# Four attention layers on one core: layer-norm statistics behind each tile's addition, normalising inside the transposing piece, and a shorter Newton step

## The chip, the core and the metric

The kernel runs on one core of one Trainium2 chip. The core has a matrix engine (TensorE, "PE" in the profile), a vector engine (VectorE, "DVE"), an activation engine (ScalarE, "ACT"), a general engine (GpSimd, "POOL") and a sync engine (SyncE, "SP") that issues nearly all DMAs of this kernel. Every engine works through its own list of instructions in order and waits at semaphores for the others. The metric is the time of the whole launch on the device, in microseconds (us); lower is better.

## The reference

The input is x, 2048 tokens of 512 numbers. Four layers follow each other; layers 0 and 2 use the weights A and a sliding window, layers 1 and 3 use the weights B and full attention. Each layer is

```
n   = (x - mean) / sqrt(var + 1e-5)          # layer norm over the 512 numbers of a token
q, k, v = split(n @ wqkv)                    # 32 heads of 16
s   = q @ k^T * 0.25                         # layers 0, 2: token i sees tokens i-255 .. i only
x   = x + softmax(s) @ v @ wo
```

and the result is x after the fourth layer. The attention itself is most of the work: 32 heads times 2048 x 2048 scores in the full layers, an eighth of that or less in the window layers.

## The kernel before

**Tiling.** Tokens are cut into four chunks of 512 (`c` = 0 to 3), each of four tiles of 128 (`i` = 0 to 3). Heads are taken in eight groups of four (`qd`) and in four groups of eight (`t` or `ht`). Operands of the projections are split in two float16 parts (high and low), so that a 512-wide product takes 12 matmuls (4 slices of the inner dimension, 3 terms). The scores are computed transposed on PE (L649), ACT takes the exponential (L653), in the window layers POOL masks the two edges (L715, L718), and PE multiplies with the values (L693 in full layers, L725 in window layers).

**The works beside the attention.** What prepares the next layer is written as works, each cut into pieces by `yield`:

- OO(l, c), `wo` (L557 to L572): loads the four x tiles of the chunk (`load_x`), then for each tile 12 matmuls (po), the scaling by gcol (dx, L567), the addition (L568) and the store to `xd` (L569); after the last tile it calls `norm`.
- `norm` (L393 to L411): for each tile bn_stats (L398) and bn_aggr (L399), then the reciprocal root of the four variances by `rsqrt` (L41 to L52: three starting operations and three Newton steps of four operations, all on 128x4), then for each tile xn (L405, float32), xh (L405, float16) and the low part (L408).
- T(l, c), `transpose` (L422 to L436): for each tile 8 PE transposes into one PSUM bank (pt, L429), a copy of the high half by ACT or DVE (L432, L434) and of the low half by DVE (L435).
- K, Q, VV: projections of the transposed chunk `xc` to keys, queries and values (48 matmuls each, pq and pv). For layer 3 they are cut into quarters, K3 and Q3 (12 matmuls).
- NN(c) (L934): the same for layer 0, whose x comes from the input. PR: preparation of a weight matrix (DVE and POOL, much of it during layer 0).

**What sets the order.** PE's order is written out when the kernel is built: the code runs under `tc.manual_schedule` for PE alone, and a planner keeps an estimated time `clock[0]`. It emits one attention step (scores, and the product of an earlier step with the values), and after a step takes pieces of the current works list until their planned share is spent. A piece may say `yield "wait", t`: then its work isn't taken again before `clock[0]` has reached t. These planned waits are not waits of the chip; they only decide where a piece stands in PE's list. On the chip PE stops where the data of the next instruction isn't there. T's first tile waits for `XNR` = the planner's time at the end of `norm` plus 10, and each further tile for 2.3 more. Behind the last chunk of a window layer come the `tails` (layer 0: OO(0,3), VV(1,2), Q(1,1), T(1,3), K(1,3); layer 2: OO(2,3), VV(3,1), VV(3,2), Q3(0,0), T(3,3), K3(3,0)), which have no attention steps between them: there the planner takes the first work of the list that is ready, and if none is, the one that is ready first, and sets its clock to that time. A projection waits 8 after its weights' load was issued (`yield wait(8)`).

The orders of DVE, ACT, POOL and SP come from a scheduler that places each instruction by its own cost estimates and the order in which the code emitted them, with `high_priority` for the copy that frees an attention bank (L599). So a change in the emission order can move instructions against each other on DVE and SP too.

**Buffers.** There are 4 x tiles (`XB`), 3 pairs of high and low parts (`XNB`), one xn, three score banks (tag "s") which the works share for their own products, and in full layers a second accumulator. A new norm may only begin when the T of the chunk before it is done.

Of the kernel before, what the change touches and what calls it, by code (L numbers as in the profile page):

```python
# [9 lines left out]
F32 = mybir.dt.float32  # L10
BF16 = mybir.dt.bfloat16
F16 = mybir.dt.float16
# [3 lines left out]
ALU = mybir.AluOpType  # L16
AX = mybir.AxisListType

S, D, H, DH, WIN = 2048, 512, 32, 16, 256
P = 128  # L20
# [13 lines left out]
EB, XB, XNB, WB, VB, OB = 6, 4, 3, 2, 3, 5  # L34
# [4 lines left out]
def rsqrt(nc, vp, tag, var):  # L39

    v = vp.tile([P, 4], F32, name=f"v{tag}", tag="lnv")  # L41
    y = vp.tile([P, 4], F32, name=f"y{tag}", tag="lny")
    z = vp.tile([P, 4], F32, name=f"z{tag}", tag="lnz")
    nc.vector.tensor_scalar_add(v, var, EPS)
    nc.vector.tensor_scalar(y.bitcast(I32), v.bitcast(I32), 1, None, op0=ALU.logical_shift_right)
    nc.vector.tensor_scalar(y.bitcast(I32), y.bitcast(I32), -1, 0x5F3759DF, op0=ALU.mult, op1=ALU.add)
    for _ in range(3):
        nc.vector.tensor_mul(z, y, y)
        nc.vector.tensor_mul(z, z, v)
        nc.vector.tensor_scalar(z, z, -0.5, 1.5, op0=ALU.mult, op1=ALU.add)  # L50
        nc.vector.tensor_mul(y, y, z)
    return y  # L52


# [135 lines left out]
def fast_path(ctx, tc, flag, a_x, a_wqkv, a_wo, b_wqkv, b_wo, out):  # L190
# [3 lines left out]
    nc = tc.nc  # L194
# [3 lines left out]
    vp = pool("work", 2)  # L198
# [7 lines left out]
            for ty in range(2) for s in range(4)}  # L206

    XC, XN, V, O, KM, EP, PH = {}, {}, {}, {}, {}, {}, {"full": False}
    CM, DN, WT, pend = {}, {}, {}, []

    clock, DONE, XNR, ONR = [0.0], {}, {}, {}

    def spent(us):
        clock[0] += us
        return us

    def wait(us):

        return "wait", clock[0] + us
# [19 lines left out]
    xd = dp.tile([NT, P, D], F32, name="xd")  # L239
# [125 lines left out]
    def weights(ty, s, n, t=None):  # L365

        w = wp.tile([P, NC, 2, D], F16, name=f"w{n}", tag="w", bufs=WB)
        if t is None:
            nc.sync.dma_start(w, wd[ty, s])
            return w  # L370
        nc.sync.dma_start(w[:, :, :, :P], wd[ty, s][:, :, :, t * P:(t + 1) * P])
        return w

    def bank(name):

        if PH["full"]:
            return acc[1]
        return ps_s.tile([P, 2, QC], F32, name=name, tag="s")[:, 0, :]
# [11 lines left out]

    def norm(l, c, xs):  # L393

        st = vp.tile([P, 4, 6], F32, name=f"st{l}_{c}", tag="st")
        mv = vp.tile([P, 4, 2], F32, name=f"mv{l}_{c}", tag="mv")
        for i in range(4):
            nc.vector.bn_stats(st[:, i, :], xs[i])  # L398
            nc.vector.bn_aggr(mv[:, i, :], st[:, i, :])  # L399
        y = rsqrt(nc, vp, f"{l}_{c}", mv[:, :, 1])  # L400
        out = []
        for i in range(4):
            xn = vp.tile([P, D], F32, name=f"xn{l}_{c}_{i}", tag="xn", bufs=1)
            xh = vp.tile([P, 2, D], F16, name=f"xh{l}_{c}_{i}", tag="xh", bufs=XNB)
            norm1 = lambda o: nc.vector.tensor_scalar(o, xs[i], mv[:, i, 0:1], y[:, i:i + 1], op0=ALU.subtract, op1=ALU.mult)  # L405
            norm1(xn)
            norm1(xh[:, 0])
            nc.vector.tensor_tensor(xh[:, 1], xn, xh[:, 0], ALU.subtract)  # L408
            out.append(xh)
        XNR[l, c] = clock[0] + (0 if (l, c) == (0, 1) else 10)  # L410
        return out  # L411

    def load_x(l, c):
        xs = []
        for i in range(4):
            k = 4 * c + i
            x = vp.tile([P, D], F32, name=f"x{l}_{k}", tag="x", bufs=XB)
            nc.sync.dma_start(x, a_x[0, k * P:(k + 1) * P, :] if l == 0 else xd[k])
            xs.append(x)
        return xs  # L420

    def transpose(l, c, xns, act):  # L422
        xc = XC[l, c] = wp.tile([P, 2, NC, QC], F16, name=f"xc{l}_{c}", tag="xc", bufs=NQ)
        for i in range(4):
            yield "wait", XNR[l, c] + 2.3 * i
            pt = bank(f"pt{l}_{c}_{i}").bitcast(F16).rearrange("p (b k n) -> p b k n", b=2, n=P)
            for b in range(2):
                for k in range(NC):
                    nc.tensor.transpose(pt[:, b, k, :], xns[i][:, b, k * P:(k + 1) * P], ident16)  # L429
            hi, lo = (xc[:, b, :, i * P:(i + 1) * P] for b in (0, 1))  # L430
            if act:
                nc.scalar.activation(hi, pt[:, 0], AF.Copy)  # L432
            else:
                nc.vector.tensor_copy(hi, pt[:, 0])  # L434
            nc.vector.tensor_copy(lo, pt[:, 1])  # L435
            yield -spent(0.6)  # L436

    def project(l, s, c, act, w=None, ht=None):


        ty, n = l % 2, f"{l}_{s}_{c}" + ("" if ht is None else f"_h{ht}")
        if not w:
            w = weights(ty, s, n, ht)
            yield wait(8)
        xc = XC[l, c]
        if s == 0:
            dst = rows(qs[ty, c])
        elif ty == 0:
            dst = rows(kw[c])
        else:  # L450
            dst = rows(kf)[:, :, c * QC:(c + 1) * QC]
        sqs = {}
        for t in range(NHT) if ht is None else (ht,):
            ps = bank(f"pq{n}_{t}")
            w0 = t * P if ht is None else 0
            yield from mms(ps, [(w[:, k, a, w0:w0 + P], xc[:, b, k, :]) for k in range(NC) for a, b in TERMS])
            settle(not sqs)
            sp = vp.tile([P, 2, QC], F16, name=f"sp{n}_{t}", tag="sp", bufs=3)
            e = es[:, ty, s, t:t + 1]
            if act:  # L460
                nc.scalar.activation(sp[:, 0], ps, AF.Copy, scale=e)  # L461
            else:
                nc.vector.tensor_scalar(sp[:, 0], ps, e, None, op0=ALU.mult)  # L463
            nc.vector.scalar_tensor_tensor(sp[:, 1], ps, e, sp[:, 0], op0=ALU.mult, op1=ALU.subtract)  # L464
            sq = vp.tile([P, QC], BF16, name=f"sq{n}_{t}", tag="sq", bufs=NHT)
            if act:
                nc.scalar.activation(sq, ps, AF.Square, scale=e)
            else:
                nc.gpsimd.tensor_tensor(sq, sp[:, 0], sp[:, 0], ALU.mult)  # L469
            sqs[t] = sq  # L470

            d = dst[8 * t:8 * t + 8].rearrange("h (d b) n -> (h d) b n", b=4)
            if s:
                nc.sync.dma_start(d[:, 0:2], sp[:, 0:1].broadcast_to([P, 2, QC]))
                nc.sync.dma_start(d[:, 2], sp[:, 1])
            else:
                nc.sync.dma_start(d[:, 0:2], sp)
                nc.sync.dma_start(d[:, 2], sp[:, 0])
            yield -MM if PH["full"] else -12 * MM
        return sqs  # L480
# [76 lines left out]
    def wo(l, c):  # L557

        w = weights(l % 2, 3, f"o{l}_{c}")
        xs = load_x(l, c)  # L560
        yield wait(8)
        for i in range(4):
            ps = bank(f"po{l}_{c}_{i}")
            yield from mms(ps, [(O[l, c, t][:, a, i * P:(i + 1) * P], w[:, t, b, :]) for t in range(NHT) for a, b in TERMS])
            d = vp.tile([P, D], F32, name=f"dx{l}_{c}_{i}", tag="xn", bufs=1)
            k = 4 * c + i
            nc.vector.tensor_tensor(d, ps, gcol[l % 2], ALU.mult)  # L567
            nc.vector.tensor_add(xs[i], xs[i], d)  # L568
            nc.sync.dma_start(out[0, k * P:(k + 1) * P, :] if l == 3 else xd[k], xs[i])  # L569
            yield -MM if PH["full"] else -12 * MM  # L570
        if l < 3:
            XN[l + 1, c] = norm(l + 1, c, xs)  # L572

    def wo_part(c, t):

# [157 lines left out]
    class Work:  # L733
# [34 lines left out]
        norm = property(lambda self: self.name is not None and self.name[0] == "N" and self.name[1] < 4)  # L768
# [89 lines left out]
    def run(g):  # L858
        for _ in g:
            pass  # L860

    def later(f, *a):

        yield from f(*a)

    pvq, late = deque(), deque()
    PT, PK, PV, PO = 2.4, 48 * MM + 0.3, 48 * MM, 48 * MM
# [34 lines left out]
        PH["full"] = False  # L902

    def T(l, c, act=True):
        return Work(later(lambda: transpose(l, c, XN.pop((l, c)), act)), PT, ("T", l, c), [("N", l, c)])

    def K(l, c, act=True):
        return Work(later(keys, l, c, act), PK, ("K", l, c), [("T", l, c), ("P", l % 2, 1), ("P", l % 2, 0)], True)
# [26 lines left out]
    def NN(c, after=()):  # L935
        def gen():
            xs = load_x(0, c)
            yield wait(12 if c > 1 else 0)
            XN[0, c] = norm(0, c, xs)
            yield 0.0  # L940
        return Work(gen(), 0.0, ("N", 0, c), after, aside=True)

# [6 lines left out]
    xs = load_x(0, 0)  # L949
    raw = {m: load_w(0, m) for m in (1, 0, 2)}  # L950
    fill(kw[0], True)
    fill(qs[0, 0], False)
    XN[0, 0] = norm(0, 0, xs)
    run(maxima(0, 1, raw[1], False))
    run(scales(0, 1))
    run(parts(0, 1, raw[1], True))
    run(maxima(0, 0, raw[0], False))
    run(transpose(0, 0, XN.pop((0, 0)), True))
    sc = scales(0, 0)
    next(sc)  # L960
    share(0)
# [109 lines left out]
```

## Time and profile before

| what | value |
|---|---|
| median of 3 runs | 2972.41 us (2970.57 to 2975.87) |
| the profiled execution | 2971.72 us, of which the span of the profile is 2970.0 us |
| PE busy | 2740.4 us (92%) |
| ACT busy | 2400.6 us (81%) |
| DVE busy | 904.0 us (30%) |
| POOL busy | 561.7 us (19%) |
| mean granted TensorE clock | 0.979 |

The stages, read off the timeline: the start with the first weights until the first scores (0 to 93 us), layer 0 (to about 615), layer 1 (to about 1605), layer 2 (to 1987), layer 3 (to the end). In a row of the timeline stand the start, the length, the engine, the line and operation, output and inputs, the number of instructions put together, and in brackets how long the engine was idle before and what released it.

### The profile page before, as it was taken

How to read it: one execution, taken by the hardware profiler on the slowest of the kernel's cores; microseconds unless marked ns; L12 is line 12 of the kernel's file. 1: busy time of each engine (PE TensorE's matmuls, PEld its weight loads, DVE VectorE, ACT ScalarE, POOL GpSimd, SP SyncE). 2: the span in 40 equal slices, each digit the busy share in tenths (PEclk: the TensorE clock that was granted, in tenths of full speed). 3: DMA queues.
4: the chain of work that ended last, by engine and by line, in shares of the span. 5: the costliest groups of instructions: out<-in, count | busy, mean ns of one | idle time of the engine just before them, and what ended most of it. 6: DMA issues, size and time to landing. Idle time of an engine off the chain costs nothing.

```text
span 2970.0 us, 52024 instructions
## 1 busy us (share of the span) xinstructions
PE 2740.4 (92%) x20314; PEld 745.7 (25%) x20314; DVE 904.0 (30%) x1914; ACT 2400.6 (81%) x2703; POOL 561.7 (19%) x1127
## 2 busy tenths in 40 slices
PE   6778889899999999999999888899999999999996
PEld 3233333321122212212212333332112211121111
DVE  7656444401113112111212455631222222222112
ACT  3454555389999999999998666639999999999996
POOL 2456564100000000000002566600000000000000
PEclk8898999999999999999999999999999999999998
DMA  6575775532223233222222756542343334333331
GB/s 212 188 227 189 237 228 172 186 107 100 77 92 104 76 115 102 92 86 93 93 102 94 228 187 184 166 135 86 127 130 123 114 126 134 123 120 122 122 114 66
DMA packets 291409, 399.35 MB, mean 134 GB/s; under 512 B 70352, under 2 KB 173264, under 8 KB 283856
## 3 DMA queue, kind: packets, MB, share of 16 engines
q1 hardware_dynamic: 291152, 395.92, 41.0%
q8 instruction: 161, 2.64, 0.4%
q14 instruction: 96, 0.79, 0.1%
HBM read 263.19 MB, written 131.60 MB: 133 GB/s over the span
## 4 chain that ended last, share of the span: by engine, by line
PE 65%; ACT 10%; DMA 10%; DVE 7%; issue 4%; POOL 2%; SPq 1%; ACTq 0%; DVEq 0%; POOLq 0%
PE acc L693 26%; PE s L649 18%; ACT e L653 9%; PE acc L385 9%; PE pq L385 4%; DMA r<-rcp 4%; PE pv L385 3%; DMA rcp<-lt 2%; PE acc L725 2%; PE po L385 2%; DMA scr<-oe 1%; POOL wr L326 1%; DMA x<-in_A_x_dram 1%; POOL w L331 1%; DVE o L626 1%
## 5 line engine op out<-in xcount | busy, mean ns | idle before, releaser
L653 ACT ACTIVATE e<-s 128x1024 f32<-128x1024 f32 (+2 forms) x2432 | 2244.0, 1113 | 173.5 <-PE s L649 156.7
L693 PE MATMUL acc<-e,vt 128*17 128x512 f32 x8192 | 1078.5, 598 | 2.8 <-DVE oe L599 2.7
L649 PE MATMUL s<-qt,kt 64*128 64x512 f16 (+3 forms) x5504 | 797.1, 356 | 88.1 <-ACT e L653 16.6
L649 PEld LDWEIGHTS <-kt 64*128 64x128 f16 x5504 | 219.1, 94 | 953.0 <-issue 928.5
L718 POOL TENSOR_SCALAR_AFFINE_SELECT e<-e 128x256 f32<-128x256 f32 x512 | 229.0, 454 | 186.4 <-ACT e L653 185.5
L599 DVE COPY oe<-acc 128x512 f32<-128x512 f32 x128 | 88.0, 687 | 510.4 <-PE acc L693 449.2
L629 POOL TENSOR_TENSOR oh<-o,oh 128x512 f16<-128x512 f32 x32 | 37.1, 1159 | 1076.6 <-DVE oh L628 1060.9
L693 PEld LDWEIGHTS acc<-e,vt 128*17 128x17 f32 x8192 | 136.4, 95 | 349.0 <-issue 322.9
L715 POOL TENSOR_SCALAR_AFFINE_SELECT e<-e 128x256 f32<-128x256 f32 x448 | 195.4, 442 | 151.1 <-ACT e L653 148.1
L385 PE MATMUL pq<-xc,w 128*128 128x512 f16 x816 | 198.3, 397 | 20.0 <-DVE dx L567 5.3
L725 PE MATMUL acc<-e,vt 128*17 128x384 f32 (+2 forms) x2816 | 203.7, 396 | 5.4 <-POOL e L715 5.3
L385 PEld LDWEIGHTS <-w 128*128 128x128 f16 x1152 | 106.5, 100 | 254.5 <-issue 161.7
L626 DVE TENSOR_TENSOR o<-o,r 128x512 f32<-128x512 f32 x64 | 51.9, 811 | 352.4 <-DMA r<-rcp 344.7
L385 PE MATMUL po<-wo,oh 128*128 128x512 f16 x444 | 113.5, 409 | 39.1 <-DVE oh L628 19.2
L461 ACT ACTIVATE sp<-pq,es 128x512 f16<-128x512 f32 x68 | 46.6, 686 | 125.5 <-PE pq L385 106.2
L469 POOL TENSOR_TENSOR sq<-sp 128x512 bf16<-128x512 f16 x28 | 29.1, 1039 | 555.8 <-DVE sp L463 555.8
L385 PE MATMUL pv<-wv,xc 128*128 128x512 f16 x576 | 129.3, 379 | 0.5 <-ACT e L653 0.5
L552 ACT ACTIVATE vt<-pv 128x512 f32<-128x512 f32 x52 | 31.1, 597 | 118.5 <-PE pv L385 118.5
L385 PEld LDWEIGHTS <-oh 128*128 128x128 f16 x768 | 68.4, 101 | 207.5 <-issue 125.0
L385 PEld LDWEIGHTS <-xc 128*128 128x128 f16 x768 | 69.8, 98 | 135.2 <-issue 62.6
L463 DVE TENSOR_SCALAR sp<-acc,es 128x512 f16<-128x512 f32 x28 | 21.0, 751 | 267.6 <-PE acc L385 231.8
L385 PE MATMUL acc<-xc,w 128*128 128x512 f16 x336 | 93.8, 383 | 3.6 <-DVE sp L464 3.6
(129 smaller groups left out, 1478.3 us busy)
## 6 DMA issues: line engine op xcount, KB each, us to landing
kt<-kf SPq DMA_DIRECT2D x128, 512.0 KB
qt<-qs SPq DMA_DIRECT2D x128, 256.0 KB
scr<-oe SPq DMA_DIRECT2D x128, 256.0 KB
xd<-x SPq DMA_DIRECT2D x96, 256.0 KB
x<-xd SPq DMA_DIRECT2D x96, 256.0 KB
w<-wd SPq DMA_DIRECT2D x22, 1024.0 KB
kt<-kw SPq DMA_DIRECT2D x64, 256.0 KB
o<-scr SPq DMA_DIRECT2D x64, 256.0 KB
```

The costliest lines, as they stand in the source:

```text
L385: nc.tensor.matmul(ps, a, b, start=(i == 0), stop=(i == len(pairs) - 1))
L461: nc.scalar.activation(sp[:, 0], ps, AF.Copy, scale=e)
L552: nc.scalar.activation(vt[:, i, :, :DH], src, AF.Copy)
L599: nc.vector.tensor_copy(oe, a)
L626: nc.vector.tensor_tensor(o, o, r, ALU.mult)
L629: (nc.gpsimd if l % 2 else nc.vector).tensor_tensor(ohl[:, 1], o, ohl[:, 0], ALU.subtract)
L649: nc.tensor.matmul(ps[:, h, s0:s0 + wd_], kt[R * h:R * h + R, pr, kc:kc + P], qt[R * h:R * h + R, pr, qc:qc + wd_], start=True, stop=True)
L653: nc.scalar.activation(e[:, :, w0:w1], ps[:, :, w0:w1], AF.Exp, scale=SCALE)
L693: nc.tensor.matmul(a[32 * h:32 * h + DH + 1, :], V[l, j // 4][:, j % 4, 4 * qd + h, :], es_[h // 2][:, h % 2, :], start=(j == 0), stop=(j ...
L715: nc.gpsimd.affine_select(v, v, pattern=[[0, 2], [-1, P]], compare_op=ALU.is_gt, fill=0.0, base=0, channel_multiplier=1)
L718: nc.gpsimd.affine_select(v, v, pattern=[[0, 2], [1, P]], compare_op=ALU.is_ge, fill=0.0, base=0, channel_multiplier=-1)
L725: nc.tensor.matmul(a[32 * h:32 * h + DH + 1, q * P:(q + nb) * P], V[l, (4 * c + j) // 4][:, j % 4, 4 * qd + h, :], es_[h // 2][:, h % 2, s ...
```

## The change

The change has five parts.

1. A Newton step takes three DVE operations instead of four; two of them are of the form (a op b) op c with a constant in the middle.
2. `norm` is split. `stats` (bn_stats and bn_aggr) is called behind each tile's addition in `wo`, and for the fourth tile also `rsqrt`, and sets `LN` = the planner's time plus 5. NN calls `stats` four times.
3. The normalising of a tile (xn, xh, low part) is emitted by `transpose`, two tiles ahead of the PE transposes that read it; the planned wait of the first tile is LN + 2, or 3 after the piece began if that is later, and the further tiles come 2 apart.
4. `load_x` in `wo` is emitted after the planned wait of 8 for the weights, not ahead of it.
5. A branch of `wo` for layer 3 that no work used is gone.

```diff
     for _ in range(3):
-        nc.vector.tensor_mul(z, y, y)
-        nc.vector.tensor_mul(z, z, v)
-        nc.vector.tensor_scalar(z, z, -0.5, 1.5, op0=ALU.mult, op1=ALU.add)
-        nc.vector.tensor_mul(y, y, z)
+        nc.vector.tensor_mul(z, y, v)
+        nc.vector.scalar_tensor_tensor(z, z, -0.5, y, op0=ALU.mult, op1=ALU.mult)
+        nc.vector.scalar_tensor_tensor(y, z, 1.5, y, op0=ALU.add, op1=ALU.mult)
...
-    def norm(l, c, xs):
...
-        XNR[l, c] = clock[0] + (0 if (l, c) == (0, 1) else 10)
-        return out
+    def stats(l, c, i, x):
+
+        if i == 0:
+            ST[l, c] = (vp.tile([P, 4, 6], F32, name=f"st{l}_{c}", tag="st"),
+                        vp.tile([P, 4, 2], F32, name=f"mv{l}_{c}", tag="mv"), [])
+        st, mv, xs = ST[l, c]
+        xs.append(x)
+        nc.vector.bn_stats(st[:, i, :], x)
+        nc.vector.bn_aggr(mv[:, i, :], st[:, i, :])
+        if i == 3:
+            del ST[l, c]
+            LN[l, c] = clock[0] + 5.0
+            XN[l, c] = (xs, mv, rsqrt(nc, vp, f"{l}_{c}", mv[:, :, 1]))
+
+    def norm(l, c, i):
+
+        xs, mv, y = XN[l, c]
+        xn = vp.tile([P, D], F32, name=f"xn{l}_{c}_{i}", tag="xn", bufs=1)
+        xh = vp.tile([P, 2, D], F16, name=f"xh{l}_{c}_{i}", tag="xh", bufs=XNB)
+        norm1 = lambda o: nc.vector.tensor_scalar(o, xs[i], mv[:, i, 0:1], y[:, i:i + 1], op0=ALU.subtract, op1=ALU.mult)
+        norm1(xn)
+        norm1(xh[:, 0])
+        nc.vector.tensor_tensor(xh[:, 1], xn, xh[:, 0], ALU.subtract)
+        return xh
...
-    def transpose(l, c, xns, act):
+    def transpose(l, c, act):
+
+        xns, ready = [], []
+        def ahead():
+            xns.append(norm(l, c, len(xns)))
+            ready.append(max([clock[0] + 1.0, LN[l, c]] + ready[-1:]) + 2.0)
+        ahead()
+        ahead()
         xc = XC[l, c] = wp.tile([P, 2, NC, QC], F16, name=f"xc{l}_{c}", tag="xc", bufs=NQ)
         for i in range(4):
-            yield "wait", XNR[l, c] + 2.3 * i
+            if ready[i] > clock[0]:
+                yield "wait", ready[i]
...
             nc.vector.tensor_copy(lo, pt[:, 1])
+            if i < 2:
+                ahead()
             yield -spent(0.6)
+        del XN[l, c]
...
     def wo(l, c):
 
         w = weights(l % 2, 3, f"o{l}_{c}")
+        yield wait(8)
+
         xs = load_x(l, c)
-        yield wait(8)
         for i in range(4):
...
-            nc.sync.dma_start(out[0, k * P:(k + 1) * P, :] if l == 3 else xd[k], xs[i])
+            nc.sync.dma_start(xd[k], xs[i])
+            stats(l + 1, c, i, xs[i])
             yield -MM if PH["full"] else -12 * MM
-        if l < 3:
-            XN[l + 1, c] = norm(l + 1, c, xs)
...
             xs = load_x(0, c)
             yield wait(12 if c > 1 else 0)
-            XN[0, c] = norm(0, c, xs)
+            for i in range(4):
+                stats(0, c, i, xs[i])
...
-    XN[0, 0] = norm(0, 0, xs)
+    for i in range(4):
+        stats(0, 0, i, xs[i])
```

More of the change, by code (lines that the diff above doesn't have):

```diff
@@ L208, in fast_path @@
     XC, XN, V, O, KM, EP, PH = {}, {}, {}, {}, {}, {}, {"full": False}
-    CM, DN, WT, pend = {}, {}, {}, []
-    clock, DONE, XNR, ONR = [0.0], {}, {}, {}
+    CM, DN, WT, ST, LN, pend = {}, {}, {}, {}, {}, []
+    clock, DONE, ONR = [0.0], {}, {}
     def spent(us):
@@ L389, in fast_path @@
     TERMS = ((0, 0), (0, 1), (1, 0))
-    def norm(l, c, xs):
[L395 to L409, printed above, removed]
-        XNR[l, c] = clock[0] + (0 if (l, c) == (0, 1) else 10)
-        return out
+    def stats(l, c, i, x):
[19 more added lines that the diff above has]
+        return xh
     def load_x(l, c):
@@ L904, in T @@
     def T(l, c, act=True):
-        return Work(later(lambda: transpose(l, c, XN.pop((l, c)), act)), PT, ("T", l, c), [("N", l, c)])
+        return Work(later(transpose, l, c, act), PT, ("T", l, c), [("N", l, c)])
     def K(l, c, act=True):
@@ L957, in fast_path @@
     run(maxima(0, 0, raw[0], False))
-    run(transpose(0, 0, XN.pop((0, 0)), True))
+    run(transpose(0, 0, True))
     sc = scales(0, 0)
```

## The prediction

> **What bounds the kernel now.** I read the page first, then the stages in windows, then the timeline of PE around each place where T stands.
>
> ```profile
> span 2970.0 us, 52024 instructions
> PE 2740.4 (92%) x20314; PEld 745.7 (25%) x20314; DVE 904.0 (30%) x1914; ACT 2400.6 (81%) x2703; POOL 561.7 (19%) x1127
> ```
>
> PE is busy 92% of the span and DVE 30%: an instruction taken off DVE is worth nothing unless PE waits for it. The windows (columns: stretch, length, then busy time and count of PE, PEld, DVE, ACT, POOL, granted clock, DMA share, GB/s) say where PE waits.
>
> ```profile
> 0.00:93.00 93.00, 53.94 (x238) 26.90 (x238) 64.83 (x136) 25.70 (x40) 18.99 (x27) 0.88 0.63 209
> 93.00:615.00 522.00, 444.94 (x3524) 187.74 (x3526) 271.36 (x569) 264.81 (x348) 253.53 (x528) 0.95 0.64 204
> 615.00:1605.00 990.00, 967.32 (x6891) 203.88 (x6892) 168.50 (x382) 949.09 (x1025) 47.46 (x46) 1.00 0.27 92
> 1605.00:1987.00 382.00, 327.82 (x2979) 135.45 (x2975) 195.72 (x448) 213.80 (x265) 195.11 (x483) 0.96 0.58 183
> 1987.00:2970.00 983.00, 946.41 (x6691) 191.78 (x6689) 203.54 (x379) 947.20 (x1025) 46.60 (x43) 0.99 0.35 115
> ```
>
> PE stands 39 us in the start, 77 in layer 0 and 54 in layer 2, but only 23 of 990 in layer 1. The change can gain or lose in the first, second and fourth window; in the full layers PE has other work while a norm runs. Layer 3's PE order is the same instruction for instruction in the two built orders, and layer 1's differs only in that T(2,c) stands some 7 us earlier. I count both as 0 (a bound of 2 each way).
>
> **Newton and statistics.**
>
> ```profile
> L49 DVE TENSOR_TENSOR z<-z,v 128x4 f32<-128x4 f32 x48 | 9.3, 194 | 1.5
> L464 DVE SCALAR_TENSOR_TENSOR sp<-pq,es,sp 128x512 f16<-128x512 f32 x68 | 50.8, 746 | 73.8 <-ACT sp L461 69.2 <-DMA qt<-qs 3.7 <-DMA qs<-sp 0.7
> ```
>
> Sixteen chunks lose 3 instructions of about 0.2 us, 9.6 us of DVE, hidden everywhere but in the start and the tails, where it is in the chains below at 0.6 us each. The new form has no 128x4 row. It lies between a two-input 128x4 operation (0.194) and the same form at 128x512 (0.746); I take 0.2, because at 4 columns the length is all fixed cost. At 0.746 the six of a chunk would add 3.3 us to a chain, 6.6 for both tails. The statistics move nowhere: in the tail quoted below, bn_stats already ran right after each addition.
>
> **The start.**
>
> ```profile
> 82.50 0.40 PE L486 MATMUL phq_None<-sq,hsum 128*32 128x512 bf16 x4
> 93.11 0.82 PE L649 MATMUL s<-qt,kt 64*128 64x384 f16 x4 [10.21 <-DMA qt<-qs]
> ```
>
> ```profile
> 83.47 3.62 DVE L285 TENSOR_REDUCE wa<-wr 128x512 f32<-128x2048 f32 x1 [3.68 <-DMA wr<-in_B_wqkv_dram]
> 87.00 0.74 DVE L517 TENSOR_SCALAR m_None<-phq_None,kx 128x512 f16<-128x512 f32 x1
> ```
>
> The first scores need qt, which needs the query shift m (L517). Its input phq is there at 82.9, but in DVE's list a maximum of layer 1's weights (wa1_1) stands ahead, which waited for its load until 83.47 and took 3.62. In the new list m stands ahead of that maximum. DVE was idle then, so m starts at 82.9 instead of 87.00: -4.1, and -0.6 for the first chunk's Newton: **-4.7**. Bounds: -7 (the weights' chain ahead is reordered too and could be 1 to 2 us shorter) and 0 (the load of qt, or POOL's weight work in layer 0, sets the pace anyway).
>
> **The tail of layer 0.** The planner waited 10 after the norm for T, and a projection waits 8 for its weights; so Q(1,1) came between. Now T waits 7 and is ready first: in the new PE list the first transposes of T(1,3) stand directly behind the last po, and Q(1,1) behind them.
>
> ```profile
> 571.57 2.75 PE L385 MATMUL pq<-xc,w 128*128 128x512 f16 x12
> 582.56 0.61 PE L429 MATMUL pt<-ident,xh 128*128 128x128 f16 x8
> 583.82 0.61 PE L429 MATMUL pt<-ident,xh 128*128 128x128 f16 x8 [0.65 <-ACT sq L467]
> 586.58 1.86 PE L429 MATMUL pt<-ident,xh 128*128 128x128 f16 x16 [2.15 <-ACT sq L467]
> 589.13 4.50 PE L385 MATMUL pq<-xc,w 128*128 128x512 f16 x12 [0.68 <-ACT xc L432]
> ```
>
> ```profile
> 571.77 0.69 DVE L567 TENSOR_TENSOR dx<-po,gcol 128x512 f32<-128x512 f32 x1 [0.23 <-PE po L385]
> 574.17 0.17 DVE L44 TENSOR_SCALAR v<-mv 128x4 f32<-128x4 f32 x1
> 578.16 0.55 DVE L405 TENSOR_SCALAR xn<-x,mv,y 128x512 f32<-128x512 f32 x1
> 579.53 0.69 DVE L408 TENSOR_TENSOR xh<-xn,xh 128x512 f16<-128x512 f32 x1
> ```
>
> In the old order 48 matmuls from 571.57 covered this chain. In the new one PE waits for it: po ends at 571.7; dx to the start of rsqrt takes 2.40 (571.77 to 574.17), rsqrt 12 x 0.2 = 2.4, xn, xh and the low part about 2.0 (578.16 to 580.2): 578.6, and PE has stood **7.0** us.
>
> After such a stop PE is slow for a while:
>
> ```profile
> 247.06 4.85 PE L385 MATMUL po<-wo,oh 128*128 128x512 f16 x12 [4.98 <-DVE dx L567]
> ```
>
> Twelve matmuls took 4.85 behind 4.98 of idling against 2.75 in the row at 571.57: +2.1. The old tail had its own stops, 0.65 + 2.15 + 0.68, and a slow group of 4.50 instead of 2.75: 5.2 that go. The three later tiles now stand between Q and K with their copies, +2 by the old stretch of 2.55 from 586.58 to 589.13. So 7.0 + 2.1 - 5.2 + 2.0 = **+5.9**; bounds +2 (the stops stay away, PE isn't slowed) and +9 (they stay).
>
> On the slow group there is a rule in the Trainium skill, page "TensorE: Matmul & The Clock Gate", section "Part 1: The HAM clock gate": after an idle window of about 3.4 us the array runs at half rate until it was busy for about as long. By that rule a stop of 7 us costs at most 1.7 more (an estimate from that page) and one of 2.15 nothing. The row at 589.13 disagrees on the second: its longest stop is 2.15, and it is slow. By the rule the sum would be about 1 us higher, since the old tail's 1.75 would have another cause and stay, and 0.8 of the two tails' slow groups would go.
>
> **T in layer 2.** T(3,0) stands three attention steps earlier in the new list.
>
> ```profile
> 1743.89 0.91 PE L649 MATMUL s<-qt,kt 64*128 64x256 f16 x8
> 1750.27 0.61 PE L649 MATMUL s<-qt,kt 64*128 64x128 f16 x8 [1.36 <-DMA qt<-qs]
> 1756.83 1.01 PE L429 MATMUL pt<-ident,xh 128*128 128x128 f16 x8 [4.96 <-DVE m_None L517]
> ```
>
> ```profile
> 1744.11 0.87 DVE L626 TENSOR_TENSOR o<-o,r 128x512 f32<-128x512 f32 x1 [3.42 <-DMA r<-rcp]
> 1747.33 0.37 DVE L44 TENSOR_SCALAR v<-mv 128x4 f32<-128x4 f32 x1
> 1752.34 0.59 DVE L405 TENSOR_SCALAR xn<-x,mv,y 128x512 f32<-128x512 f32 x1
> 1754.53 0.68 DVE L408 TENSOR_TENSOR xh<-xn,xh 128x512 f16<-128x512 f32 x1
> ```
>
> DVE's chain doesn't start earlier: an output tile (L626) holds it until 1744.11. Its 15 small operations take 5.0 here; 12 take 4.0, so the low part is ready at 1754.2. PE comes to the transposes where it now begins the step at 1743.89, and would wait 10.3 in place of 4.96 + 1.36; I take 1 off because the three steps that now follow don't stop again: **+3**, bounds 0 and +6.
>
> ```profile
> 1837.52 0.40 PE L429 MATMUL pt<-ident,xh 128*128 128x128 f16 x4 [3.46 <-DVE xh L405]
> ```
>
> ```profile
> 1916.48 1.04 PE L649 MATMUL s<-qt,kt 64*128 64x384 f16 x8 [6.10 <-DVE xc L435]
> ```
>
> ```profile
> 1912.81 0.69 DVE L626 TENSOR_TENSOR o<-o,r 128x512 f32<-128x512 f32 x1 [4.21 <-DMA r<-rcp]
> ```
>
> T(3,1) waits 3.46 for a norm that is 3 x 0.36 shorter now: **-1.1**. At T(3,2) the bank copies stood behind L626, which waited for its DMA to 1912.81, and PE lost 6.10. In the new order its tiles stand two steps earlier, one per step, and two of the three copies no longer stand behind L626; I let 2.7 of the 6.10 stay, for the third: **-3.4**; bounds -6 and 0. T(1,2) in layer 0 is like it:
>
> ```profile
> 505.66 0.61 PE L429 MATMUL pt<-ident,xh 128*128 128x128 f16 x8 [2.92 <-DVE xc L435]
> ```
>
> Half of that goes: **-1.5** (0 to -3).
>
> **The tail of layer 2.** The same turn as in layer 0: T(3,3) stands behind the last po, VV(3,2) ahead of it and Q3(0,0) behind it.
>
> ```profile
> 1944.36 8.89 PE L385 MATMUL po<-wo,oh 128*128 128x512 f16 x39 [0.51 <-DVE oh L628]
> 1953.08 10.52 PE L385 MATMUL pv<-wv,xc 128*128 128x512 f16 x48
> 1969.15 1.05 PE L429 MATMUL pt<-ident,xh 128*128 128x128 f16 x16 [1.26 <-ACT sq_h L467]
> ```
>
> ```profile
> 1953.28 0.69 DVE L567 TENSOR_TENSOR dx<-po,gcol 128x512 f32<-128x512 f32 x1 [0.23 <-PE po L385]
> 1960.05 0.69 DVE L408 TENSOR_TENSOR xh<-xn,xh 128x512 f16<-128x512 f32 x1
> ```
>
> The 10.52 that covered the chain are spent earlier. From po's end, 1953.2, the chain takes to 1960.7 - 0.6 less one second-tile operation, about 1959.6: PE stops 6.4, is slow for 2.1, and some 1.8 of the later stops go: **+6.7**; bounds +3 and +9.
>
> **SP.** load_x stands later in SP's list, behind other stores. A late x tile would hold the addition, DVE's whole list behind it, and then PE.
>
> ```profile
> L568 DVE TENSOR_TENSOR x<-x,dx 128x512 f32<-128x512 f32 x48 | 35.2, 734 | 1.3
> ```
>
> The 48 additions waited 1.3 us in all, so the loads had slack, and they can't start before the x tiles come free anyway. I take 0; bounds 0 and +8 (two waits for a DMA like the 4.21 at 1912.81).
>
> **Sum.** -4.7 - 1.5 + 5.9 + 3 - 1.1 - 3.4 + 6.7 = +4.9. The profiled execution took 2971.72, its span 2970.0, and the median is 0.7 above it: 2972.4 + 4.9 = about **2977**. What a measurement can tell from no change is about 0.2%, 5.9 us; the sum lies just within.
>
> **Rivals.** (a) Slower: the start's gain is swallowed. In layer 0 pauses end by DVE's and POOL's weight preparation, such as the 4.98 at 247.06; if that work, and not the attention, sets those times, the first scores can come 4.7 earlier and layer 0 still ends when it did. Then the sum is +9.6, about 2982; it needs only that 1.1 or more of the 4.7 is lost to be slower by 0.2%. For it: DMA at 0.64 and POOL at 254 of 522 us there; against it: POOL follows attention's masks in order. (b) Faster: the window layers' pauses shrink, since the norm's 12 large operations of a chunk no longer stand as one block in DVE's list ahead of L567, L626 and L435. Of the 77 + 54 us, 13 (a tenth) would have to go to give 2964; it decides from 11 on. For it: pauses released by DVE in every row of T above; against it: many of those end by a DMA or by a weight cast. (c) The change does nothing that can be seen: the scheduled order moves, each stop is replaced by another of its length: 2972. Against it: the tails' two stops are written into PE's list.
>
> **Chances.** My sum (2973 to 2981) 0.45, of which 0.27 is within 0.2% and 0.18 above; (a) 0.25, slower; (b) 0.23, faster; (c) 0.07, within. So faster 0.23, same 0.34, slower 0.43. The range reaches from (b) to the tails' upper bounds on top of (a): 2962 to 2989. The likeliest case alone is 2973 to 2981.
>
> **What would show it.** In the new profile: the first scores at about 88; the first transposes of both tails behind 6 to 7 us of idling released by xh, with a slow matmul group after; T(3,0) behind 8 to 10; no stop of 6 at T(3,2); small operations at 0.2 in the new form. Wrong it would be by a different set of pauses in layer 0, which I can't order by hand, or by an x load that comes late.

## The result and the profile after

The changed kernel takes 2988.22 us (median of 10 runs, 2983.82 to 2997.57) against 2973.93 us before (10 runs, 2970.57 to 2981.7): a ratio of 1.0049, 95% interval 1.0034 to 1.0063. It is slower by some 14 us. The profiled execution took 2987.40 us, 15.7 more than that of the kernel before. The first lines of its page:

```profile
span 2985.6 us, 51970 instructions
PE 2752.5 (92%) x20314; PEld 749.5 (25%) x20314; DVE 892.5 (30%) x1866; ACT 2400.7 (80%) x2703; POOL 560.5 (19%) x1127
```

DVE does 11.5 us less, most of it by the shorter Newton step, and PE is busy 12.1 us longer with the same 20314 matmuls: they run slower. The windows, cut at the same events as before (columns as in the prediction):

```profile
0.00:85.00 85.00, 55.17 (x238) 27.87 (x238) 62.20 (x128) 25.72 (x40) 19.35 (x27) 0.90 0.67 223
85.00:618.00 533.00, 452.29 (x3522) 189.64 (x3522) 269.23 (x553) 264.78 (x348) 251.49 (x528) 0.93 0.63 201
618.00:1608.00 990.00, 968.48 (x6891) 202.99 (x6892) 166.16 (x373) 949.84 (x1025) 47.47 (x46) 1.00 0.27 92
1608.00:2003.00 395.00, 330.66 (x2976) 137.14 (x2973) 191.31 (x433) 213.20 (x265) 195.57 (x483) 0.94 0.57 177
2003.00:2986.00 983.00, 945.90 (x6692) 191.83 (x6690) 203.60 (x379) 947.16 (x1025) 46.62 (x43) 0.99 0.35 115
```

The start is 8 us shorter, layer 0 is 11 us longer (533 against 522) and layer 2 is 13 (395 against 382); the full layers keep their 990 and 983. In both window layers the granted clock is 0.02 lower.

To see where, I follow one event through both traces: the copy that frees an attention bank (L599 before, L614 after). It comes 128 times, in the same order in every kernel here, so the time of the n-th copy less its time in the kernel before is the lag at that place. The table gives it in us at eight of these copies, named by their time in the kernel before; it has all runs that the text reads from it.

| copy at | changed | loadx_ first | newton_ alone | before_ wait7 | wait10_ tails | tails_ back | wait13_ vv | copies_ first | wait13_ copies |
|---|---|---|---|---|---|---|---|---|---|
| 276 | -10.2 | -9.1 | -6.0 | 2.8 | -10.5 | -8.6 | -9.8 | -9.7 | -5.2 |
| 499 | -6.5 | -8.2 | -4.7 | 3.3 | -6.3 | -2.9 | -14.3 | -15.8 | -13.0 |
| 545 | -1.7 | -2.9 | -1.5 | 6.0 | 0.8 | 3.6 | -11.2 | -10.7 | -9.7 |
| 647 (behind tail 0) | 3.2 | -1.2 | -1.6 | 9.5 | -1.6 | -1.2 | -12.0 | -5.9 | -13.8 |
| 1606 (layer 2 begins) | 2.7 | 1.4 | -1.2 | 16.6 | 0.1 | -0.9 | -11.9 | -5.7 | -13.9 |
| 1841 | 7.9 | 4.3 | 0.5 | 14.1 | 6.2 | 6.9 | -2.6 | -0.3 | -10.4 |
| 1931 (ahead of tail 2) | 8.1 | 3.0 | -1.6 | 19.9 | 6.2 | 4.6 | -2.8 | -0.9 | -11.4 |
| 2020 (behind tail 2) | 16.3 | 11.3 | -1.4 | 27.3 | 13.3 | 5.5 | -0.7 | 7.2 | -9.2 |

Each column is one execution. loadx_first has the changed kernel's PE order from end to end and yet stands up to 5 us from it (11.3 against 16.3 at 2020 us), so a difference of up to 5 between columns proves nothing by itself, and a smaller step within a column is what that one execution showed. The changed kernel wins 10 in the start and the first chunk, loses 8.5 in layer 0's later chunks, 5 in the first tail (1.7 in loadx_first), 5 in layer 2 and 8 in the second tail.

The start in the changed kernel, PE and then DVE:

```profile
79.47 0.40 PE L501 MATMUL phq_None<-sq,hsum 128*32 128x512 bf16 x4
85.47 1.04 PE L664 MATMUL s<-qt,kt 64*128 64x384 f16 x6 [5.59 <-DMA qt<-qs]
```

```profile
79.93 0.75 DVE L532 TENSOR_SCALAR m_None<-phq_None,kx 128x512 f16<-128x512 f32 x1 [2.12 <-PE phq_None L501]
80.62 3.62 DVE L284 TENSOR_REDUCE wa<-wr 128x512 f32<-128x2048 f32 x1
```

The query shift stands ahead of the weights' maximum and runs as soon as phq is there; the first scores come at 85.47 instead of 93.11. The tail of layer 0:

```profile
559.22 10.05 PE L384 MATMUL po<-wo,oh 128*128 128x512 f16 x39 [3.14 <-DVE oh L643]
575.15 0.61 PE L441 MATMUL pt<-ident,xh 128*128 128x128 f16 x4 [5.88 <-DVE xh L411]
576.61 4.07 PE L384 MATMUL pq<-xc,w 128*128 128x512 f16 x12
590.83 0.61 PE L441 MATMUL pt<-ident,xh 128*128 128x128 f16 x8 [1.05 <-DVE xc L447]
592.12 4.68 PE L384 MATMUL pq<-xc,w 128*128 128x512 f16 x12 [0.69 <-ACT xc L444]
```

```profile
569.30 0.69 DVE L583 TENSOR_TENSOR dx<-po,gcol 128x512 f32<-128x512 f32 x1 [0.23 <-PE po L384]
571.70 0.17 DVE L44 TENSOR_SCALAR v<-mv 128x4 f32<-128x4 f32 x1
574.09 0.55 DVE L411 TENSOR_SCALAR xn<-x,mv,y 128x512 f32<-128x512 f32 x1
575.47 0.68 DVE L414 TENSOR_TENSOR xh<-xn,xh 128x512 f16<-128x512 f32 x1
```

PE waits 5.88 for xh behind the last po, and the 12 matmuls that follow take 4.07. The tail of layer 2:

```profile
1938.23 20.89 PE L384 MATMUL pv<-wv,xc 128*128 128x512 f16 x96
1958.96 10.52 PE L384 MATMUL po<-wo,oh 128*128 128x512 f16 x48
1975.36 0.61 PE L441 MATMUL pt<-ident,xh 128*128 128x128 f16 x4 [5.88 <-DVE xh L411]
1976.81 3.71 PE L384 MATMUL pq_h<-xc,w_h 128*128 128x512 f16 x12
1990.26 13.25 PE L384 MATMUL pv<-wv,xc 128*128 128x512 f16 x48 [0.51 <-DMA wv<-wd]
```

Both groups of values (96 matmuls) run ahead of po, the stop of 5.88 comes behind it, and the last group of 48 takes 13.25 instead of 10.5. Between the tails stand the transposes of the window layers, T(1,2), T(3,0) and T(3,1):

```profile
493.44 0.91 PE L441 MATMUL pt<-ident,xh 128*128 128x128 f16 x12
495.01 0.40 PE L441 MATMUL pt<-ident,xh 128*128 128x128 f16 x4 [0.66 <-DVE xh L414]
499.74 0.61 PE L664 MATMUL s<-qt,kt 64*128 64x256 f16 x4 [4.01 <-DVE xc L447]
508.55 0.40 PE L664 MATMUL s<-qt,kt 64*128 64x384 f16 x4 [1.89 <-DVE xc L447]
1754.56 0.61 PE L441 MATMUL pt<-ident,xh 128*128 128x128 f16 x4 [7.57 <-DVE xh L411]
1776.23 4.22 PE L384 MATMUL pv<-wv,xc 128*128 128x512 f16 x12 [2.58 <-ACT sq_h L482]
1844.43 0.40 PE L441 MATMUL pt<-ident,xh 128*128 128x128 f16 x4 [2.47 <-DVE xh L411]
1851.38 0.61 PE L664 MATMUL s<-qt,kt 64*128 64x128 f16 x4 [2.81 <-DVE xc L447]
```

At T(1,2) the transposes of two tiles now stand in a row (16, from 493.44), so two banks wait for DVE, which copies them (L447) only behind the normalising of the later tiles:

```profile
498.58 0.77 DVE L414 TENSOR_TENSOR xh<-xn,xh 128x512 f16<-128x512 f32 x1
499.28 0.74 DVE L447 COPY xc<-pt 128x512 f16<-128x512 f16 x2
```

### The profile page after: what moved, and what is told of

The parts are those of the page before. It is cut to its first block, busy times and chain, and to the rows that moved or that the text cites. A ratio compares the mean times of both kernels' runs of the same rounds, so it can differ in the third digit from the quotient of the medians.

```text
span 2985.6 us, 51970 instructions
## 1 busy us (share of the span) xinstructions
PE 2752.5 (92%) x20314; PEld 749.5 (25%) x20314; DVE 892.5 (30%) x1866; ACT 2400.7 (80%) x2703; POOL 560.5 (19%) x1127
## 4 chain that ended last, share of the span: by engine, by line
PE 66%; ACT 10%; DMA 8%; DVE 8%; issue 4%; POOL 2%; SPq 1%; ACTq 0%; DVEq 0%; POOLq 0%
PE acc L708 26%; PE s L664 18%; PE acc L384 9%; ACT e L668 9%; PE pq L384 4%; PE pv L384 4%; DMA r<-rcp 4%; DMA rcp<-lt 2%; PE acc L740 2%; PE po L384 2%; POOL wr L325 1%; POOL w L330 1%; DMA scr<-oe 1%; DVE o L641 1%; DVE xh L411 1%
## 5 line engine op out<-in xcount | busy, mean ns | idle before, releaser
L614 DVE COPY oe<-acc 128x512 f32<-128x512 f32 x128 | 88.1, 688 | 522.1 <-PE acc L708 455.8
```

Of the source, the lines that this page charges most:

```text
L614: nc.vector.tensor_copy(oe, a)
```

## The experiments

Two theories. A: the shorter planned wait costs, since T's transposes now stand in PE's list before their norm is done. B: the normalising's new place costs, since it stands on DVE ahead of other work. The ratios are to the kernel before, run beside each of them (4 to 10 runs of each changed kernel).

| run | median, us | ratio | 95% interval |
|---|---|---|---|
| newton_alone | 2975.63 | 0.9989 | 0.9971 to 1.0007 |
| loadx_first | 2990.23 | 1.0049 | 1.0029 to 1.0068 |
| before_wait7 | 3001.58 | 1.0091 | 1.0068 to 1.0115 |
| wait10_tails | 2985.94 | 1.0022 | 1.0006 to 1.0039 |
| tails_back | 2976.91 | 0.9994 | 0.9978 to 1.0010 |
| wait10_vv | 2974.45 | 0.9992 | 0.9976 to 1.0008 |
| wait13_vv | 2970.12 | 0.9974 | 0.9960 to 0.9988 |
| wait16_vv | 2982.41 | 1.0001 | 0.9980 to 1.0021 |
| before_wait13 | 2993.12 | 1.0042 | 1.0026 to 1.0058 |
| newton_wait13 | 2983.25 | 1.0023 | 1.0005 to 1.0041 |
| copies_first | 2979.34 | 1.0007 | 0.9996 to 1.0017 |
| wait13_copies | 2963.07 | 0.9949 | 0.9927 to 0.9972 |

**The Newton step alone.** The kernel before with the first hunk of the diff.

> The kernel before with the three-operation Newton step alone. Nine of the operations at 0.2 us instead of twelve: 0.6 us per chunk, exposed only in the start and at the few transposes of layer 2 that PE waits for, so -1 to -3, about 2971 to 2973. If the scheduler moves other work with it, up to 5 either way; the first scores are expected at 92.5, so if they come 7 us earlier, the start's gain is Newton's.

The first scores came 4.3 earlier, in this kernel's PE and DVE rows:

```profile
81.17 0.40 PE L485 MATMUL phq_None<-sq,hsum 128*32 128x512 bf16 x4
88.83 0.82 PE L648 MATMUL s<-qt,kt 64*128 64x384 f16 x4 [7.26 <-DMA qt<-qs]
```

```profile
81.62 0.75 DVE L516 TENSOR_SCALAR m_None<-phq_None,kx 128x512 f16<-128x512 f32 x1 [2.84 <-PE phq_None L485]
82.29 3.61 DVE L284 TENSOR_REDUCE wa<-wr 128x512 f32<-128x2048 f32 x1
```

I had expected 0.6 from three fewer operations. The turn of m and the weights' maximum on DVE, which I had put down to the change as a whole, is the scheduler's answer to the shorter Newton step alone; 1.3 of the 4.3 is phq, which also came earlier (81.17 against 82.50). Of the time 0.1% is left, inside the measurement.

**Where load_x stands.** In the changed kernel:

```diff
-        yield wait(8)
-
         xs = load_x(l, c)
+        yield wait(8)
```

> The changed kernel with load_x emitted ahead of the planned wait again, as in the kernel before. If the later x loads cost nothing, as forecast, the time stays within 2 us of the changed kernel, 2986 to 2990; if a late x tile holds an addition, up to 8 us below it.

It measured the changed kernel's own ratio, 1.0049, with an interval of 0.2% to each side: no cost of the later x loads can be seen.

**The waits alone.** In the kernel before:

```diff
-        XNR[l, c] = clock[0] + (0 if (l, c) == (0, 1) else 10)
+        XNR[l, c] = clock[0] + (0 if (l, c) == (0, 1) else 7)
...
-            yield "wait", XNR[l, c] + 2.3 * i
+            yield "wait", XNR[l, c] + 2.0 * i
```

> The kernel before with the planned waits alone changed: 7 in place of 10 for the first transposes and 2.0 in place of 2.3 between tiles; norm, Newton and loads as they were. Theory A: both tails get the stop, +5.6 in layer 0 and +9 in layer 2, about 2986 to 2990, without the start's gain of 7.6 even more. Theory B: the tails lose, but the transposes in the window layers stay as cheap as before, so the lag over the kernel before grows only at the two tails and is 0 up to 560 us. If the lag grows elsewhere too, the waits and not the place of the normalising cause it.

Slower by 0.91%, nearly twice the changed kernel's loss and more than theory A had said. The table of lags shows that it grows everywhere: 6 up to 545 us, 3.5 in the first tail, 7 in layer 1, 3 in layer 2 and 7.4 in the second tail. So the wait costs by itself, as theory A says, and in the window layers too, which speaks against B as the only cause. From 276 to 2020 us the two kernels lose nearly the same, 24.5 here and 26.5 in the changed kernel, though not at the same places (layer 1 costs 7 here and nothing there); what keeps the changed one faster than this is the start.

**The tails' wait put back.** In the changed kernel:

```diff
-            LN[l, c] = clock[0] + 5.0
+            LN[l, c] = clock[0] + (8.0 if l % 2 and c == 3 else 5.0)
```

> The changed kernel with the planned wait of the last chunk's transposes in the two tails put back to 10 (LN + 8 + 2), so that in the tail of layer 0 the 48 query matmuls stand ahead of the transposes again, and in the tail of layer 2 the 12 matmuls of Q3(0,0) do; the values VV(3,2) still stand ahead of po in layer 2. Theory A (the planned wait of 7 against the projections' 8 causes the tails' loss): layer 0's tail wins back about 5.6 us and layer 2's some 3 of its 9, so 8 to 9 us below the changed kernel, about 2979. Theory B (the loss sits in DVE's new order, the normalising beside the copies that free banks, and the tails would lose it at another place): less than 3 us, about 2986 or more.

0.27% or 8 us below the changed kernel by the ratios, 3 between the two traces at 2020 us. In the first tail the queries run behind po again and the stop of 5.88 is gone; the tail now gains 2.4 where it lost 4.9:

```profile
571.10 2.75 PE L384 MATMUL pq<-xc,w 128*128 128x512 f16 x12
584.79 0.61 PE L441 MATMUL pt<-ident,xh 128*128 128x128 f16 x8 [1.43 <-DVE xc L447]
```

The second still loses 7.1; its rows:

```profile
1936.27 20.89 PE L384 MATMUL pv<-wv,xc 128*128 128x512 f16 x96
1967.36 2.75 PE L384 MATMUL pq_h<-xc,w_h 128*128 128x512 f16 x12
1973.93 0.40 PE L441 MATMUL pt<-ident,xh 128*128 128x128 f16 x4 [3.82 <-DVE xh L411]
```

The 96 matmuls still stand ahead of po. The wait of T(3,3) isn't what moved VV(3,2): by the code only two works may hold their weights at a time (WB is 2), and since T(3,2) now ends earlier in the plan, VV(3,2) takes the second place before OO(2,3) does. before_wait7, in which only the waits differ, has the same 96 in a row (20.89 us from 1950.04).

**The values put back too.** The run before, with the weights of VV(3,2) not before the output tiles that OO(2,3) needs:

```diff
-             2: [OO(2, 3), VV(3, 1), VV(3, 2), Q3(0, 0, True), T(3, 3), K3(3, 0, True)]}
+             2: [OO(2, 3), VV(3, 1), VV(3, 2, more=[("O", 2, 3, NHT - 1)]), Q3(0, 0, True), T(3, 3), K3(3, 0, True)]}
```

> The run with the tails' wait of 10 (wait10_tails), and in layer 2's tail the values VV(3,2) held behind po as in the kernel before, so both tails have the kernel before's PE order. In wait10_tails the tail of layer 2 still lost 7.2 us. Theory A (PE's order of the tails alone makes their loss: 10.5 us of matmuls no longer cover the norm's chain): those 7.2 go, to about 2979 against 2986 of wait10_tails; what is left over the kernel before sits in the transposes of the window layers. Theory B (the tail of layer 2 loses by DVE's order or by slow matmuls whatever PE's order): it stays at 2984 or more.

```profile
1957.50 10.52 PE L384 MATMUL pv<-wv,xc 128*128 128x512 f16 x48
1967.86 2.75 PE L384 MATMUL pq_h<-xc,w_h 128*128 128x512 f16 x12
1970.45 1.06 PE L441 MATMUL pt<-ident,xh 128*128 128x128 f16 x16
```

The stop ahead of the transposes is gone, the second tail costs 0.9 in place of 7.1, and the time is that of the kernel before. The tails' PE order alone is 0.55% or 16 us by the ratios and 10.8 between the two traces at 2020 us: within the intervals as much as the whole loss.

**Longer waits everywhere.** tails_back with LN set to the planner's time plus 8 (wait10_vv), 11 (wait13_vv) and 14 (wait16_vv) for all chunks, that is planned waits of 10, 13 and 16.

> As tails_back, with the planned wait of 10 for every chunk's first transposes, not the tails' alone. The shorter Newton step, the normalising in the transposing piece and the start's gain stay. Theory A (the shorter wait is the loss): the transposes of layer 2 stop 5 to 8 us less, and the time is below the kernel before, about 2968 to 2973. Theory C (normalising inside the transposing piece costs in the window layers by itself, since copies that free banks stand behind more DVE work): no better than tails_back, about 2977 to 2980.

> As wait10_vv with a planned wait of 13. Theory A: the norm's chain takes about 7 us on a quiet DVE and 10 where it is held by an output tile's DMA, so 13 covers T(3,0) and T(3,1) too: 2 to 5 us below wait10_vv. Theory C: no change, or worse by the later keys and queries behind.

> As wait13_vv with a planned wait of 16. If stops of the transposes were still to be covered, 1 to 3 us below wait13_vv; if the optimum is passed, the keys and queries behind come too late and it is 2 us or more slower than wait13_vv, about equal to the kernel before.

10 is no better than tails_back, against theory A; 13 is faster than the kernel before by 0.26%; 16 is back at that kernel's time. Of the three, 13 is the best, but the step from 10 to 13 (0.18%) lies inside the two intervals, and that from 13 to 16 (0.27%) hardly outside. With 13, the start's gain reaches layer 2 undiminished (-11.9 at 1606 us).

**The same wait without the split.** XNR plus 13 in the kernel before, and with the Newton step:

> The kernel before with a planned wait of 13 in place of 10 ahead of the first transposes, nothing else. If the wait is the lever by itself, it wins here too what it won between 10 and 13 in the changed kernel (4 to 5 us): about 0.15% below the kernel before. If the gain of the 13 belongs to the new place of the normalising (emitted later, with the transposing piece, it then comes in time), this run is no faster than the kernel before, 0 to +3.

> The same with the three-operation Newton step: 1 to 3 us below before_wait13, from the start (first scores 4.3 earlier in newton_alone, of which 1.4 was left at the end). If it equals wait13_vv (0.26% below the kernel before), the split of the norm and its place in the transposing piece are worth nothing beside the wait and the Newton step; if it is 3 us or more slower, the split is worth that.

Both are slower than the kernel before, by 0.42% and 0.23%; neither of the expected outcomes for before_wait13 holds, and the Newton step's 0.19% between the two (1 to 3 us were expected) lies inside the intervals. The kernel before was best at 10 of the three waits tried (7, 10, 13). By number, the split of the norm is worth 0.49% at 13 (0.9974 against 1.0023) and nothing at 10 (0.9992 against 0.9989 of newton_alone).

But the same number isn't the same place. In the kernel before the wait counts from the end of `norm`, which the planner takes one piece after the last addition; in the changed kernel it counts from that addition itself. The table counts, in the traces, the PE matmuls between the last po of a chunk and the first transposes of its T, for the T that have attention steps between (T(2,0) to T(2,2) are left out: their output tiles stand under a name, acc, that other products share):

| T | before (10) | before_ wait7 | before_ wait13 | changed (7) | wait10_ vv | wait13_ vv | wait16_ vv |
|---|---|---|---|---|---|---|---|
| T(1,0) | 96 | 96 | 232 | 144 | 108 | 108 | 196 |
| T(1,1) | 108 | 84 | 256 | 108 | 108 | 256 | 256 |
| T(1,2) | 108 | 108 | 144 | 108 | 108 | 108 | 144 |
| T(2,3) | 104 | 104 | 120 | 132 | 132 | 132 | 132 |
| T(3,0) | 148 | 124 | 172 | 72 | 124 | 148 | 172 |
| T(3,1) | 132 | 108 | 156 | 132 | 132 | 132 | 156 |
| T(3,2) | 168 | 144 | 192 | 96 | 96 | 120 | 144 |

At T(3,0) and T(3,1) the split form with 13 stands where the kernel before stands with 10, and with 16 where before_wait13 stands. So the 0.49% compares different places. Paired by those two rows, wait13_vv is 0.15% below newton_alone, and wait16_vv 0.22% below newton_wait13, both inside the intervals; the other rows don't pair. So it isn't shown that the split is worth something. Nor is theory B's plain form shown, that the normalising's new place costs by itself: no pair has a loss.

**The copies ahead of the normalising.** In the changed kernel, and in wait13_vv:

```diff
-            nc.vector.tensor_copy(lo, pt[:, 1])
+            with tc.high_priority(HEAD_START):
+                nc.vector.tensor_copy(lo, pt[:, 1])
```

> The changed kernel with the copy of the low half (L447), which frees a transpose's bank, given the priority that the copy of an attention bank has, so that DVE's order puts it ahead of the normalising of later tiles where it is ready. If the window layers' loss (7 us at T(1,2) and T(1,1) in layer 0, 2.5 at T(3,1)) comes from copies standing behind normalising, the stops released by xc at 499 and 508 us (4.01 and 1.89) and at 1851 (2.81) shrink, and the time is 4 to 8 us below the changed kernel, 2980 to 2984. If it comes from the transposes' own wait for the norm, which is then merely seen at the next bank, nothing changes: 2986 to 2990.

> The same edit on the run with a planned wait of 13 and the tails' old order. There the transposes come later, so fewer copies should be behind a norm: 0 to 4 us below wait13_vv, 0.26 to 0.4% below the kernel before; if equal or slower, the copies' place isn't what is left.

The time fell, by 0.42% or 12 us, more than the 4 to 8 of the first expectation, and not at the stops that it named. At T(1,2) DVE's order didn't change, and the stops are there as before; at T(3,1) it did, and the stop is 2.81 again (1843.19 us):

```profile
490.40 0.61 PE L665 MATMUL s<-qt,kt 64*128 64x256 f16 x4 [4.01 <-DVE xc L448]
499.54 0.40 PE L665 MATMUL s<-qt,kt 64*128 64x384 f16 x4 [2.08 <-DVE xc L448]
```

The gain lies between 276 and 499 us (-15.8 against -6.5 of the changed kernel), where DVE's order did change, at T(1,0) and T(1,1) and in the additions of OO(0,1). PE's order is the changed kernel's throughout, so DVE's order alone carries the gain, as theory B has it for a wait of 7; whether it is the copies or the additions that moved with them wasn't tried. wait13_copies is 0.51% faster than the kernel before (2963.07 us), the best version found; over wait13_vv that is 0.25%, more than the 0 to 4 us expected and no wider than the intervals.

## Why the prediction was right or wrong

Direction and range were right: 2977 within 2962 to 2989 was said, slower as the likeliest of the three, and 2988.22 measured. The point was 11 us short, and that the range held, by less than 1 us, is in part luck: by 276 us the start had won 5.5 more than its 4.7, and the window layers ahead of their tails cost about 17 more than their terms (8.5 and 5.4 lost where I had -1.5 in each), so that one error hid a third of the other. Of the 0.43 for slower, 0.25 stood on rival (a). In the predicted steps:

- **The start, -4.7.** Measured -7.64 at the first scores. The turn of m on DVE is as told (some 4 of it; newton_alone, with 1.3 from phq, has 4.3); that phq itself comes 3.0 earlier, 79.47 against 82.50, was named only in the bound of -7.
- **Newton's new form, 0.2 us.** Right; the groups of the changed kernel:

```profile
L49 DVE SCALAR_TENSOR_TENSOR z<-z,y 128x4 f32<-128x4 f32 x48 | 9.3, 195 | 1.6
L50 DVE SCALAR_TENSOR_TENSOR y<-z,y 128x4 f32<-128x4 f32 x48 | 9.6, 199 | 1.6
```

- **The tail of layer 0, +5.9.** Measured +4.9 between the copies around it, with 5.88 of waiting for 7.0: PE starts on the high half and doesn't wait for the low part. The slow group of 4.50, which the sum let go, came again (4.68 at 592.12, but 2.99 in loadx_first). The cause of the stop, T's 7 against the projections' 8, is shown by wait10_tails.
- **The tail of layer 2, +6.7.** Measured +8.2. The stop was 5.88 for 6.4; the matmuls behind were slower than the 2.1 counted (13.25 for 10.5 in the last group alone). The size was near and the cause half wrong: not T(3,3)'s wait but T(3,2)'s earlier end, through the weights' two places, moved the values ahead of po.
- **T in the window layers, -1.5 at T(1,2), +3 at T(3,0), -1.1 at T(3,1), -3.4 at T(3,2).** This is the step that failed. Up to the tail, layer 0 gave back 8.5 where I had -1.5, 4.8 of it at T(1,2) (from -6.5 to -1.7) and the rest between 276 and 499 us, for which I had no term, only the warning that pauses in layer 0 might come otherwise; T(3,0) cost 4.9 and T(3,1) 2.4 (lags of copies that the table leaves out: 3.0 at 1731 us, 7.9 at 1829, 10.4 at 1887). I reckoned with what a shorter chain saves and with L626, and at T(3,1) the first stop did shrink as I had it (3.46 to 2.47). I didn't reckon with the second tile: by the code its wait, too, has run out by the time T's turn comes, so its transposes stand directly behind the first's, meet an unready norm and hold two banks until DVE, still normalising, copies them. 2.92 became 4.01 and 1.89 at T(1,2), and at T(3,1) 1.71 of the kernel before became 2.81. T(3,2) gave -2.3 for -3.4.

```profile
1844.25 0.61 PE L429 MATMUL pt<-ident,xh 128*128 128x128 f16 x8 [1.71 <-DVE xc L435]
```

- **Layers 1 and 3, 0.** Right: -0.5 from 647 to 1606 us, and 16.3 at every copy of layer 3.
- **load_x, 0.** Right, by loadx_first.
- **Rival (a)** ended at about the right time by a mechanism that isn't there: at 276 us, behind the weight preparation's longest stops, the start's gain was still 10.2, and wait13_vv carries it through two layers. **Rival (b)** didn't happen in the changed kernel; copies_first, 0.42% below it by DVE's order alone, shows that pauses of its kind can shrink by as much.
- **The clock.** A stop of 5.88 was followed by 12 matmuls in 4.07 and 3.71, +1.3 and +1.0 against the 2.1 of the row chosen; with the same PE order and the same stop, loadx_first had 4.98 and copies_first 5.29 (+2.2 and +2.5), so the price differs from execution to execution. The prediction's estimate from the Trainium skill, "TensorE: Matmul & The Clock Gate", "Part 1: The HAM clock gate", 1.7 at most behind an idle window of some 3.4 us, covers the first two and not the others. It doesn't give the 13.25 at 1990 us either, behind stops of no more than 2.15 since 1977 us.

What stays open: why T(3,0) costs 4 us in newton_alone as well, whose PE order there is the kernel before's, and whether both forms of the norm have the same best place for T, since 10 in the one and 13 in the other put T(3,0) and T(3,1) at the same place.

## What to carry to other kernels

A planned wait in a written order is a tuned number: it decides not only when a piece may come but which of two works comes first, and here 7 against 8 took away the matmuls that had hidden a chain of 6 us. When a chain is made shorter or split, keep the order that hid it, look for every limit that the earlier piece now reaches first (here, the two places for weights), check from which event the wait counts, and sweep it again; with the wait at 13, the tails' old order and the copies in front, the same change is 0.5% faster than the kernel before.

## What the runs showed that I had not expected

Removing three 0.2 us operations from a chain on DVE moved the first scores by 4.3 us, because the scheduler's order turned. And PE's slow stretches don't need a long stop: the last 48 matmuls ahead of layer 3 took 13.25 us in the changed kernel, behind stops of 2.15 and 0.51, 12.22 in tails_back, with the stop of 2.15 alone directly ahead, and 10.53 in the kernel before, where that stop stands ahead of them too. What decides between these isn't shown. The rows of the kernel before:

```profile
1976.39 0.38 PE L486 MATMUL phk<-sq_h,hsum 128*32 128x512 bf16 x1 [2.15 <-ACT sq_h L467]
1976.69 10.53 PE L385 MATMUL pv<-wv,xc 128*128 128x512 f16 x48
```
